# First loads on the software DMA queue, first FFN steps by token tile, and more transposes on TensorE in a linear-attention + SwiGLU kernel

## The chip, the cores and the metric

The kernel runs on one core of a Trainium2 chip. The metric is the device time of one execution in microseconds (us). The engines of the core are TensorE (PE), VectorE (DVE), ScalarE (ACT), GpSimd (POOL) and SyncE (SP). DMAs are issued by SP (hardware queue) or by POOL (software queue). PEld is PE's loading of weights.

## The reference

Cosine-weighted linear attention over 8 batches, 8 heads, 576 positions and 64 dimensions, then RMS normalization and a SwiGLU feed-forward network (FFN) with 512 model and 1536 inner dimensions on the 4608 tokens:

```python
q_p = phi(q, cos_w, sin_w)      # phi: concat(relu(x)*cos, relu(x)*sin): 128 features
k_p = phi(k, cos_w, sin_w)
kv  = einsum('bhsf,bhsd->bhfd', k_p, v);  z = sum(k_p, axis=2)
x   = einsum('bhsf,bhfd->bhsd', q_p, kv) / (einsum('bhsf,bhf->bhs', q_p, z) + 1e-06)
xn  = x / sqrt(mean(x * x) + 1e-06) * rms_g
out = (silu(xn @ w_gate) * (xn @ w_val)) @ w_out
```

All inputs and the output are float32; the kernel multiplies in bf16.

## The kernel before, in words

Each batch has 512 "main" tokens (four tiles `j` of 128) and 64 rest tokens; the rest tokens of all batches make a ninth FFN block, `xnT8`. The order of the work is written out by hand: every engine executes its instructions in the order of the program text.

**Attention of a batch.** `load_piece` brings `raw` (q, k or v; 1 MB) and the 64 rest rows (`remq`, `remk`, `remv`). `q_prep(b, j)` scales a tile by cos and sin into `qp` and transposes it into `qpT`, either with a DMA transpose on SP or, with `on_pe`, by eight PE transposes into a PSUM tile and a copy. `k_prep` and `v_prep` fill `kp` and `vv`. `kvz(b, half)` is 20 matmuls per half and a copy to `kvzs`. `nd(b, j)` makes numerator and denominator of tile `j` in PSUM (pool `att`). `x_of(b, j)` computes `den`, `rec` and `xt` on DVE, the sum of squares (`scr`, `ssq`) on ACT, and `ms` and `rs` on POOL. `xn` scales the tile on DVE and transposes it into `xnT`, by DMA or (`xn_pe`, and the head's `xn0`) by four PE transposes into `tpx` and a copy on ACT. `qr_prep` and `nd(b, NJ)` do the rest tokens of two batches at a time.

**FFN of a block.** `gval(blk, nn)`, twelve steps: four gate matmuls (`gps`) and four value matmuls (`vps`), 512 tokens wide, then `sil` on ACT and `hT` on DVE. `outp` (for block 0 the loop behind L474) accumulates over the twelve `hT` into `acc`; `store` copies it to `osb` (three buffers) on ACT and issues the output DMA on SP.

**Order.** The head loads batch 0 on SP, lets POOL wait for v (`gate`) before the weights, and does the attention of batch 0. Then come the twelve steps of block 0 with batch 1's scaling beside them, the output phase of block 0 with batch 1's attention, and blocks 1 to 8. In block `blk`, `attention_beside(blk + 1, nn)` and its two companions place the work of the next three batches beside step `nn`; block 1 has no `outp`.

Of the kernel before, what the change touches and what calls it, by code (L numbers as in the profile page):

```python
# [10 lines left out]
FP32 = mybir.dt.float32  # L11
# [6 lines left out]
def kernel(  # L18
# [28 lines left out]
    EPS = 1e-6  # L47

# [6 lines left out]
    xt_pool = ctx.enter_context(tc.tile_pool(name="xt", bufs=5))  # L55
# [13 lines left out]
    vv = consts.tile([P, NJ + 1, H, DE], BF16, name="vv")  # L69
    qpT = consts.tile([P, H, SM], BF16, name="qpT")  # L70
# [16 lines left out]
    def load_piece(what, src, b, h0, n, eng):  # L87
# [58 lines left out]
    def q_prep(b, j, e_cos=nc.vector, e_sin=nc.vector, on_pe=False):  # L146
# [3 lines left out]
        if on_pe:  # L150
            tps = pools["tps"].tile([P, H, P], BF16, name="tps", tag="tps")
            for h in range(H):
                nc.tensor.transpose(tps[:, h, :], qp[:, h, :], ident[:, :])
            return tps
# [37 lines left out]
    xts = {}  # L192
    xnTs = {}
# [20 lines left out]
    def x_of(b, j):  # L214
# [9 lines left out]
        xt = xt_pool.tile([P, DM], FP32, name="xt", tag="xt")  # L224
        nc.vector.tensor_tensor(  # L225
            out=xt[:, :].rearrange("p (g h d) -> p g h d", g=2, d=D),
# [4 lines left out]
        scr = ffn_pool.tile([P, DM], BF16, name="scr", tag="scr", bufs=1)  # L231
        ssq = small.tile([P, 1], FP32, name="ssq", tag="ssq")
        nc.scalar.activation(out=scr[:, :], in_=xt[:, :], func=AF.Square, accum_out=ssq[:, :])  # L233
        ms = small.tile([P, 1], FP32, name="ms", tag="ms")
        nc.gpsimd.tensor_scalar(  # L235
            out=ms[:, :], in0=ssq[:, :], scalar1=1.0 / DM, scalar2=EPS, op0=ALU.mult, op1=ALU.add
        )
        rs = small.tile([P, 1], FP32, name="rs", tag="rs")
        nc.gpsimd.tensor_tensor(out=rs[:, :], in0=ms[:, :], in1=mhalf[:, :], op=ALU.pow)  # L239
        xts[b, j] = (xt, rs)  # L240

    def xn(b, j, tps=None):
        xt, rs = xts.pop((b, j))
        if j < NJ:
            if b not in xnTs:
                xnTs[b] = xnt_pool.tile([P, NDT, SM], BF16, name="xnT", tag="xnT")
            dst, col = xnTs[b], j
        else:
            xnTs[B] = xnT8
            dst, col = xnT8, b // 2  # L250
        t = xn_pool.tile([P, DM], BF16, name="xn", tag="xn")
        nc.vector.scalar_tensor_tensor(  # L252
            out=t[:, :], in0=xt[:, :], scalar=rs[:, 0:1], in1=gb[:, :], op0=ALU.mult, op1=ALU.mult
        )
        if tps is not None:
            for dt in range(NDT):
                nc.tensor.transpose(tps[:, dt, :], t[:, dt * P : (dt + 1) * P], ident[:, :])  # L257
        else:
            nc.sync.dma_start_transpose(out=dst[:, :, col * P : (col + 1) * P], in_=t[:, :])
# [82 lines left out]
    for s in range(0, DFF, 512):  # L342
        load_wgv(s)
# [195 lines left out]
```

## Time and profile before

| | |
|---|---|
| median of 3 runs | 384.48 us (379.05 to 385.63) |
| profiled execution | 384.23 us, its span 382.5 us |
| PE busy | 325.6 us (85%) |
| DVE busy | 199.5 us (52%) |
| ACT busy | 147.9 us (39%) |
| POOL busy | 101.8 us (27%) |
| chain that ended last | PE 61%, DMA 12%, DVE 9%, issue 7%, POOL 5%, ACT 3% |
| granted PE clock, mean | 0.959 |
| moved by DMA | 54.65 MB, of them HBM read 38.01, written 9.44 |

Times in the rows are us from the span's start. A row of the timeline has start, duration, engine, source line, operation, output and input, count, and in brackets how long the engine stood idle before it and what released it. SPq and POOLq rows are the issuing of DMAs. The chain of work that ended last follows each instruction back to what released it; a DMA in it lasts from its issue to its landing.

### The profile page before, as it was taken

The page shows a single profiled execution, that of the slowest core. Times are in us where ns is not written, and L with a number is a line of the kernel's source. Part 1 is how long each engine was busy: PE and PEld are TensorE (multiplying, and loading weights), DVE is VectorE, ACT ScalarE, POOL GpSimd, SP SyncE. Part 2 cuts the span into 40 slices and gives each one's busy share as a digit, 9 for nine tenths or more (in the row PEclk, how much of TensorE's full clock was granted, in tenths as well). Part 3 has the DMA queues.
Part 4 walks back from the last instruction along what each step waited for, and adds up shares of the span by engine and source line. Part 5 has one row for each costly group of instructions (what it writes and reads, how often), then busy time and mean ns, then how long its engine had stood idle before and what let it go on. Part 6 is the DMA issues. An engine that isn't in the chain of part 4 may idle for free.

```text
span 382.5 us, 5536 instructions
## 1 busy us (share of the span) xinstructions
PE 325.6 (85%) x1979; PEld 158.2 (41%) x2016; DVE 199.5 (52%) x426; ACT 147.9 (39%) x295; POOL 101.8 (27%) x176
## 2 busy tenths in 40 slices
PE   0456996569855799989999997999999999999995
PEld 0342443233422254445445543444454444444442
DVE  2653592529467426963784684568737422222210
ACT  2724360435333434443445342534534433233221
POOL 0428410380046005731570375037002000000000
PEclk9999999996965799999999999899999999999999
DMA  7899999169055604896699289969902210000113
GB/s 224 211 204 235 291 322 251 38 203 277 1 137 147 130 29 110 166 225 161 164 235 247 74 172 174 164 157 208 240 27 70 55 55 28 27 29 38 45 48 92
DMA packets 69181, 54.65 MB, mean 143 GB/s; under 512 B 50688, under 2 KB 58368, under 8 KB 69152
## 3 DMA queue, kind: packets, MB, share of 16 engines
q0 software_dynamic: 12192, 29.50, 32.1%
q1 hardware_dynamic: 56816, 24.52, 29.1%
q8 instruction: 16, 0.26, 0.3%
q10 hardware_dynamic: 144, 0.26, 0.2%
q14 instruction: 13, 0.11, 0.1%
HBM read 38.01 MB, written 9.44 MB: 124 GB/s over the span
## 4 chain that ended last, share of the span: by engine, by line
PE 61%; DMA 12%; DVE 9%; issue 7%; POOL 5%; ACT 3%; SPq 2%; ACTq 0%; DVEq 0%; POOLq 0%
PE vps L273 19%; PE gps L273 19%; PE acc L303 17%; DMA raw<-in_v_dram 6%; DMA qpT<-qp 5%; DVE xt L225 2%; PE kvz L181 2%; PE nd L208 2%; DVE xn L252 2%; POOL raw L91 2%; POOL rs L239 2%; DMA out_dram<-osb 1%; DVE hT L279 1%; DVE kp L124 1%; SPq L98 1%
## 5 line engine op out<-in xcount | busy, mean ns | idle before, releaser
L279 DVE TENSOR_TENSOR hT<-vps,sil 128x512 bf16<-128x512 f32 x108 | 74.3, 688 | 137.2 <-PE vps L273 97.0
L273 PE MATMUL vps<-xnT,wv 128*128 128x512 bf16 x379 | 104.3, 399 | 3.6 <-ACT osb L285 3.2
L273 PE MATMUL gps<-xnT,wg 128*128 128x512 bf16 x366 | 101.3, 396 | 6.0 <-ACT sil L278 3.3
L303 PE MATMUL acc<-wo,hT 128*128 128x512 bf16 x374 | 96.2, 381 | 0.6
L278 ACT ACTIVATE sil<-gps 128x512 bf16<-128x512 f32 x108 | 63.9, 592 | 76.3 <-PE gps L273 73.1
L273 PEld LDWEIGHTS <-wv 128*128 128x128 bf16 x432 | 43.8, 101 | 59.2 <-issue 11.8
L273 PEld LDWEIGHTS <-wg 128*128 128x128 bf16 x432 | 40.8, 101 | 50.1 <-issue 11.5
L303 PEld LDWEIGHTS <-hT 128*128 128x128 bf16 x384 | 37.7, 98 | 46.2 <-issue 1.4
L235 POOL TENSOR_SCALAR ms<-ssq 128x1 f32<-128x1 f32 x36 | 7.3, 203 | 169.8 <-ACT scr L233 169.8
L233 ACT ACTIVATE scr<-xt 128x512 bf16<-128x512 f32 x36 | 22.7, 630 | 70.0 <-DVE xt L225 69.0
L285 ACT COPY osb<-acc 128x512 f32<-128x512 f32 x36 | 20.8, 585 | 30.6 <-PE acc L303 25.0
L252 DVE SCALAR_TENSOR_TENSOR xn<-xt,rs,gb 128x512 bf16<-128x512 f32 x36 | 26.6, 743 | 2.1 <-POOL rs L239 2.1
L225 DVE TENSOR_TENSOR xt<-nd,rec 128x512 f32<-128x512 f32 x36 | 24.9, 691 | 1.2
L131 ACT CAST vv<-raw 128x512 bf16<-128x512 f32 x28 | 16.0, 623 | 17.3 <-DMA raw<-in_v_dram 17.3
L239 POOL TENSOR_TENSOR rs<-ms,mhalf 128x1 f32<-128x1 f32 x36 | 21.0, 582 | 3.0
L257 PE MATMUL tpx<-ident,xn 128*128 128x128 bf16 x48 | 6.2, 272 | 17.0 <-DVE xn L252 17.0
L181 PE MATMUL kvz<-vv,kp 128*128 128x65 bf16 x320 | 14.1, 199 | 7.4 <-DVE vv L133 3.4
L208 PE MATMUL nd<-kvzs,qpT 128*128 128x65 bf16 x256 | 14.5, 202 | 5.7 <-DVE xt L225 3.0
L208 PEld LDWEIGHTS <-qpT 128*128 128x128 bf16 x256 | 12.8, 103 | 14.3 <-issue 5.6
L124 DVE TENSOR_SCALAR qp<-raw,cos_tab 128x512 bf16<-128x512 f32 x32 | 15.1, 477 | 5.7 <-DMA raw<-in_q_dram 5.7
L181 PEld LDWEIGHTS <-kp 128*128 128x128 bf16 x320 | 12.9, 101 | 11.5 <-issue 3.6
L91 POOL DMA_DIRECT2D raw<-in_k_dram x22 | 17.0, 772 | 2.3 <-DVE kp L124 2.3
(59 smaller groups left out, 225.6 us busy)
## 6 DMA issues: line engine op xcount, KB each, us to landing
out_dram<-osb SPq DMA_DIRECT2D x32, 256.0 KB, 3.6
raw<-in_q_dram POOLq DMA_DIRECT2D x20, 256.0 KB, 6.8
raw<-in_k_dram POOLq DMA_DIRECT2D x20, 256.0 KB, 3.8
raw<-in_v_dram POOLq DMA_DIRECT2D x20, 256.0 KB, 4.3
raw<-in_q_dram POOLq DMA_DIRECT2D x2, 1024.0 KB, 11.8
raw<-in_k_dram POOLq DMA_DIRECT2D x2, 1024.0 KB, 13.0
raw<-in_v_dram POOLq DMA_DIRECT2D x2, 1024.0 KB, 15.5
wg<-in_moe_w_gate_dram POOLq DMA_DIRECT2D x3, 512.0 KB, 9.0
```

The lines of the kernel that those rows point to most:

```text
L91: eng.dma_start(out=raws[what, b][:, h0 : h0 + n, :], in_=src[b, h0 : h0 + n, 0:SM, :].rearrange("h (p j) d -> p h (j d)", j=NJ),)
L181: nc.tensor.matmul(ps[:, half, hh * DE : (hh + 1) * DE], lhsT=kp[:, c, h, :], rhs=vv[:, c, h, :], start=(c == 0), stop=(c == NJ),)
L208: nc.tensor.matmul(ps[rows, h // HH, (h % HH) * DE : (h % HH + 1) * DE], lhsT=src[:, h, cols], rhs=kz[:, h, :], start=True, stop=True,)
L225: nc.vector.tensor_tensor(out=xt[:, :].rearrange("p (g h d) -> p g h d", g=2, d=D), in0=ndv[:, :, :, 0:D], in1=rec[:, :].rearrange("p (g h ...
L233: nc.scalar.activation(out=scr[:, :], in_=xt[:, :], func=AF.Square, accum_out=ssq[:, :])
L239: nc.gpsimd.tensor_tensor(out=rs[:, :], in0=ms[:, :], in1=mhalf[:, :], op=ALU.pow)
L252: nc.vector.scalar_tensor_tensor(out=t[:, :], in0=xt[:, :], scalar=rs[:, 0:1], in1=gb[:, :], op0=ALU.mult, op1=ALU.mult)
L273: nc.tensor.matmul(ps[:, :], lhsT=w[:, dt, nn * P : (nn + 1) * P], rhs=xnT[:, dt, :], start=(dt == 0), stop=(dt == NDT - 1),)
L278: nc.scalar.activation(out=sil[:, :], in_=gps[:, :], func=AF.Silu)
L279: nc.vector.tensor_tensor(out=hT[:, nn, :], in0=vps[:, :], in1=sil[:, :], op=ALU.mult)
L285: nc.scalar.copy(out=osb[:, :], in_=acc[:, :])
L303: nc.tensor.matmul(acc[:, :], lhsT=hTs[blk][:, nn, j * P : (j + 1) * P], rhs=wo[:, nn, :], start=(nn == 0), stop=(nn == NNT - 1),)
```

## The change

Five edits. (1) The first loads: half of batch 0's q stays on SP in two pieces, the other half, k, v and the weights go to POOL's queue, without the wait for v; the gain vector goes from ACT to SP; `load_rest` makes the rest rows a DMA of its own. (2) FFN steps 0 and 1 of block 0 are computed tile by tile: `first_steps(j)` does both steps for the 128 tokens of tile `j` right after that tile's transposes. (3) Batch 1's q tiles are transposed on PE, and its scaled `xn` tiles wait one step before PE transposes them; the same for batch 2's `xn` tiles, in a placement of its own (`batch2_beside`), with half of batch 2's q and k scaling on ACT. Batch 1's rest tokens move from the output phase to block 1. (4) `ms` goes: `xt` has a 513th column with the constant sqrt(EPS*512), the square is scaled by 512**-0.5, and `rs` is one power on POOL. `xt` is a ring of five fixed tiles. (5) The head's PSUM pools of its own go: `gv`, `acc` and `att` (one buffer) are used from the start.

The diff, cut:

```diff
-        if h0 + n == H:
...
+    def load_rest(what, src, b, eng):
+        lane = 64 * (b % 2) if what == "q" else 0
+        t = rem_pool.tile([P, H, D], FP32, name="rem" + what, tag="rem" + what)
+        eng.dma_start(
+            out=t[lane : lane + SR, :, :], in_=src[b, :, SM:S, :].rearrange("h s d -> s h d")
+        )
+        raws[what + "r", b] = t
...
+    def q_tr_pe(b, j, eng):
+        qp = qps.pop((b, j))
+        tps = pools["acc"].tile([P, H, P], BF16, name="tps", tag="acc")
+        for h in range(H):
+            nc.tensor.transpose(tps[:, h, :], qp[:, h, :], ident[:, :])
+        copy(eng, qpT[:, :, j * P : (j + 1) * P], tps[:, :, :])
...
-        nc.gpsimd.tensor_scalar(
-            out=ms[:, :], in0=ssq[:, :], scalar1=1.0 / DM, scalar2=EPS, op0=ALU.mult, op1=ALU.add
+        nc.scalar.activation(
+            out=scr[:, :], in_=xt[:, :], func=AF.Square, scale=DM**-0.5,
+            accum_out=ssq[:, :],
         )
-        nc.gpsimd.tensor_tensor(out=rs[:, :], in0=ms[:, :], in1=mhalf[:, :], op=ALU.pow)
+        nc.gpsimd.tensor_tensor(out=rs[:, :], in0=ssq[:, :], in1=mhalf[:, :], op=ALU.pow)
...
+    def gval_mm(blk, nn, c0, n):
...
+        for ps, w in zip(gv_ps[blk, nn], (wg, wv)):
             for dt in range(NDT):
                 nc.tensor.matmul(
-                    ps[:, :], lhsT=w[:, dt, nn * P : (nn + 1) * P], rhs=xnT[:, dt, :],
-                    start=(dt == 0), stop=(dt == NDT - 1),
+                    ps[:, c0 : c0 + n], lhsT=w[:, dt, nn * P : (nn + 1) * P],
+                    rhs=xnTs[blk][:, dt, c0 : c0 + n], start=(dt == 0), stop=(dt == NDT - 1),
                 )
...
+    load_piece("q", q, 0, 0, 2, nc.sync)
+    load_piece("q", q, 0, 2, 2, nc.sync)
+    load_piece("q", q, 0, HH, HH, nc.gpsimd)
...
+    load("k", k, 0)
+    load("v", v, 0)
...
+    xn_scale(0, 1)
+    xn_tr_pe(0, 1)
+    first_steps(0)
+    x_of(0, 3)
+    xn_scale(0, 2)
+    xn_tr_pe(0, 2)
+    first_steps(1)
+    xn_scale(0, 3)
+    xn_tr_pe(0, 3)
+    first_steps(2)
+    first_steps(3)
+    gval_end(0, 0)
+    gval_end(0, 1)
...
+        if 8 <= r <= 11:
+            xn_tr_pe(2, r - 8)
+        if 7 <= r <= 10:
+            xn_scale(2, r - 7)
+        if 6 <= r <= 9:
+            nd(2, r - 6)
+            x_of(2, r - 6)
...
-        if 5 <= nn <= 8:
-            q_prep(1, nn - 5)
+        if 6 <= nn <= 9:
+            q_scale(1, nn - 6, V, A)
+        if 8 <= nn <= 11:
+            q_tr_pe(1, nn - 8, V if nn % 2 else A)
```

**POOL at the start of the program**, before (`gate` reads v and so waits for it; `wg` and `wv` are the weights):

```order
L320 IOTA iota_i 128x1
masks.py:197 MEMSET ident 128x128
masks.py:199 AFFINE_SELECT ident<-ident 128x128
L341 COPY gate<-raw 128x1
L108 DMA wg<-in_moe_w_gate_dram 128x4x512
L108 DMA wv<-in_moe_w_val_dram 128x4x512
```

and POOL at the same place now:

```order
L91 DMA raw<-in_q_dram 128x4x256
L359 ISA
L359 IOTA iota_i 128x1
masks.py:197 MEMSET ident 128x128
masks.py:199 AFFINE_SELECT ident<-ident 128x128
L91 DMA raw<-in_k_dram 128x8x256
L100 DMA remk<-in_k_dram 64x8x64
L91 DMA raw<-in_v_dram 128x8x256
L100 DMA remv<-in_v_dram 64x8x64
L114 DMA wg<-in_moe_w_gate_dram 128x4x512
L114 DMA wv<-in_moe_w_val_dram 128x4x512
```

Half of q stands ahead of the iota and the identity, k and v behind them, and the weights follow at once.

**SP from its first load to batch 2's q**, before (`qpT` of four tiles is batch 1's, of eight batch 2's and batch 3's; `xnT_102` holds the rest tokens):

```order
L91 DMA raw<-in_q_dram 128x8x256
L98 DMA remq<-in_q_dram 64x8x64
L91 DMA raw<-in_k_dram 128x8x256
L98 DMA remk<-in_k_dram 64x8x64
L91 DMA raw<-in_v_dram 128x4x256 x2
L98 DMA remv<-in_v_dram 64x8x64
L155 DMA_TRANSPOSE qpT<-qp 128x8x128 x4
L166 DMA_TRANSPOSE qprT<-qpr 128x8x128
L288 DMA out_dram<-osb 128x512 x4
L259 DMA_TRANSPOSE xnT_102<-xn 128x4x128
L155 DMA_TRANSPOSE qpT<-qp 128x8x128 x8
```

and SP's rows now, to the same place:

```order
L91 DMA raw<-in_q_dram 128x2x256 x2
L363 DMA gb<-in_moe_rms_g_dram 128x512
L184 DMA_TRANSPOSE qprT<-qpr 128x8x128
L332 DMA out_dram<-osb 128x512 x4
L162 DMA_TRANSPOSE qpT<-qp 128x8x128 x4
L281 DMA_TRANSPOSE xnT_104<-xn 128x4x128
L162 DMA_TRANSPOSE qpT<-qp 128x8x128 x4
```

Batch 1's four q transposes are gone from SP; batch 2's still stand behind the four stores of block 0, and the rest tokens' transpose has moved behind them.

**DVE in the second half of block 1**, a step of the loop before (`hT` of the step, then tile 2 of batch 2, then batch 3's q and k):

```order
L279 TENSOR_TENSOR hT<-vps,sil 128x512
L218 TENSOR_SCALAR den<-nd 128x8
L223 RECIPROCAL rec<-den 128x8
L225 TENSOR_TENSOR xt<-nd,rec 128x512
L252 SCALAR_TENSOR_TENSOR xn<-xt,rs,gb 128x512
L124 TENSOR_SCALAR qp<-raw,cos_tab 128x8x64
L124 TENSOR_SCALAR qp<-raw,sin_tab 128x8x64
L124 TENSOR_SCALAR kp<-raw,cos_tab 128x8x64
L124 TENSOR_SCALAR kp<-raw,sin_tab 128x8x64
```

and a step at the same place now:

```order
L319 TENSOR_TENSOR hT<-vps,sil 128x512
L266 SCALAR_TENSOR_TENSOR xn<-xt_96,rs,gb 128x512
L237 TENSOR_SCALAR den<-nd 128x8
L242 RECIPROCAL rec<-den 128x8
L245 TENSOR_TENSOR xt_97<-nd,rec 128x512
L130 TENSOR_SCALAR qp<-raw,cos_tab 128x8x64
L130 TENSOR_SCALAR qp<-raw,sin_tab 128x8x64
L130 TENSOR_SCALAR kp<-raw,cos_tab 128x8x64
L130 TENSOR_SCALAR kp<-raw,sin_tab 128x8x64
```

`xn` stands ahead of `den` to `xt`. It scales the tile of the step before, and PE transposes it one step later still; before, PE's transposes in a step took the `xn` of that same step.

More of the change, by code (lines that the diff above doesn't have):

```diff
@@ L149, in q_prep, with q_tr @@
         relu_scaled(e_sin, qp[:, :, D:F], main("q", b, j), sin_tab, j, slice(0, P))
[L150 to L154, printed above, removed]
+        qps[b, j] = qp
+    def q_tr(b, j):
+        qp = qps.pop((b, j))
         nc.sync.dma_start_transpose(
@@ L449, in attention_beside @@
             x_of(b, NJ)
[L450 to L452 removed]
+        if 4 <= r <= 7:
             xn(b, r - 4)
```

262 lines of the change are left out of this document (138 added, 124 removed).

## The prediction

> **What bounds the kernel now.** I read the busy time by phases first, then the chain of work that ended last and the timeline in the phases where TensorE (PE) waits.
>
> ```profile
> 34.00:56.00 22.00, 21.73 (x93) 9.62 (x95) 13.47 (x27) 9.37 (x16) 9.79 (x13) 1.00 1.09 304
> 56.00:80.00 24.00, 15.66 (x152) 8.15 (x153) 11.66 (x28) 8.58 (x21) 6.24 (x13) 1.00 0.61 138
> 80.00:129.00 49.00, 33.66 (x181) 15.01 (x185) 29.10 (x65) 18.06 (x38) 16.45 (x27) 0.76 0.66 168
> 128.98:382.00 253.02, 243.36 (x1436) 116.24 (x1463) 128.50 (x260) 96.78 (x195) 57.60 (x100) 0.99 0.52 116
> ```
>
> The window rows give the busy time of PE, its weight loads, VectorE (DVE), ScalarE (ACT) and GpSimd (POOL), then granted clock, DMA share and GB/s. From 129 us on PE is busy 243.4 of 253.0 us: nothing there is to be had but its waits. What can move lies before: 34 us until the first gate matmul (33.95 below), 24 us for batch 0's output phase with PE busy 15.7, and 49 us for block 1 at a clock of 0.76. The change touches just these, so I sum them phase by phase.
>
> ```profile
> 9.08 1.33 ACT L122 ACTIVATE qp<-raw,sin_tab 128x512 bf16<-128x512 f32 x2 [6.21 <-DMA raw<-in_q_dram]
> 15.39 1.01 ACT L131 COPY qpT<-tps 128x1024 bf16<-128x1024 bf16 x1 [1.37 <-PE tps L153]
> 18.76 1.13 ACT L131 CAST vv<-raw 128x512 bf16<-128x512 f32 x2
> 22.86 0.43 DVE L133 CAST kvzs<-kvz 128x260 bf16<-128x260 f32 x1 [3.31 <-PE kvz L181]
> 33.95 0.58 PE L273 MATMUL gps<-xnT,wg 128*128 128x512 bf16 x1 [0.67 <-ACT xnT L131]
> 39.03 1.03 PE L273 MATMUL gps<-xnT,wg 128*128 128x512 bf16 x4
> 41.79 0.86 PE vps L273 x4
> 4.00:14.00 10.00, 2.42 (x22) 2.16 (x23) 2.36 (x5) 3.55 (x5) 0.00 (x0) 1.00 1.10 331
> 14.77 0.95 POOL L108 DMA_DIRECT2D wg<-in_moe_w_gate_dram  x1
> 16.00:18.00 2.00, 0.00 (x0) 0.10 (x1) 2.00 (x5) 2.00 (x4) 2.00 (x3) 1.00 0.57 61
> 35.00:37.00 2.00, 2.00 (x6) 0.72 (x5) 0.00 (x0) 0.60 (x1) 2.00 (x4) 1.00 1.02 399
> ```
>
> **Head, to FFN step 2 (39.03 us before).** ACT works without a long pause from q's landing (9.08) to the last vv cast (19.89): 10.8 us, of which q's part ends at 16.40, 7.3 us after q landed. v's landing does not set the end. Two things shorten it. First, q's 1 MB goes over two queues and only 512 KB of it shares SP's. The DMA engines are full from 4 to 14 us in both kernels (331 GB/s, share 1.10), so total bytes come hardly sooner, and 399 GB/s on POOL's queue at 35 us is the most it may gain. But q now stands ahead of everything: about 0.5 MB by 4 us, the whole by 5, and as before about 2 us from last bytes to the compute, so 7 instead of 9.08. Second, three scalings now precede the first transposes, and ACT's four (0.66 us each) no longer alternate with its copies: q's part takes about 5.9 us. So it ends at 12.9 (16.40 before). The k and v parts on ACT (3.5 us, 16.40 to 19.89) start at once if k has landed: q, gain vector and k are 2.3 MB, 9.3 us plus 2, so 11.3. They end at 16.5, **−3.3 us**. Bounds: 0 (the loads land as before and hide it) and −5 (k at 9.5).
>
> On POOL's queue the first half of q goes ahead of iota and identity (about 0.8 us later, idle until q lands), and k, v and the weights follow without the wait for v. The rest of q stands behind all weights and v's landing (about 14.5); the four rs behind it are wanted only past 22. The five one-column memsets lie in DVE's idle time before q. The gain vector moves to SP and is wanted past 22 too.
>
> From the last kvzs copy (23.29) to step 2 it took 15.74 us. Call this point T. By hand, with one `att` buffer instead of two: nd and the normalization chain of the four tiles end with xn of tile 3 at about T+9.3 as before (the missing ms saves 0.27 per tile, by 157.04 below; the single buffer gives it back). New is that steps 0 and 1 run under that wait: each tile brings 16 matmuls of 128 columns, 1.8 us cold (4 cold ones of that width take 0.61 at 110.48 below, with their tail) and 1.0 warm. Tiles 0 and 1 are hidden; behind the last transposes stand tiles 2 and 3. Step 2 starts at T+12.6, **−3.1 us**; if the narrow matmuls cost 1.6 each, −1.9.
>
> **FFN of batch 0, steps 2 to 11.** PE is the bound (21.73 of 22). Added are 4 times 8 transposes; 4 warm ones take 0.40 with their tail (72.75 below), so 8 take 0.5: **+2.0 us**, or 3.8 at half clock. The copies (0.69 on DVE, 1.01 on ACT) and the sines moved to ACT fit: ACT has 9.37 of 22 in use, and its fullest step holds 0.6 + 0.66 + 1.01 = 2.3 us against PE's 2.2.
>
> ```profile
> 56.30 0.81 PE L480 MATMUL acc<-wo,hT 128*128 128x512 bf16 x3
> 47.77 17.42 DMA qpT<-qp
> 60.12 0.77 PE L181 MATMUL kvz<-vv,kp 128*128 128x65 bf16 x20
> 62.22 0.43 DVE L133 CAST kvzs<-kvz 128x260 bf16<-128x260 f32 x1 [3.57 <-PE kvz L181]
> 65.24 0.43 PE L208 MATMUL nd<-kvzs,qpT 128*128 128x65 bf16 x8 [2.26 <-DMA qpT<-qp]
> 70.45 0.42 PE L208 MATMUL nd<-kvzs,qpT 128*128 128x65 bf16 x8 [0.45 <-DVE xt L225]
> 72.75 0.40 PE L257 MATMUL tpx<-ident,xn 128*128 128x128 bf16 x4 [1.88 <-DVE xn L252]
> 80.16 1.02 PE L273 MATMUL gps<-xnT,wg 128*128 128x512 bf16 x4 [0.30 <-ACT osb L285]
> 80.13 5.28 DMA out_dram<-osb
> 86.15 1.86 PE L273 MATMUL vps<-xnT,wv 128*128 128x512 bf16 x4 [3.24 <-ACT osb L285]
> ```
>
> **Output phase of batch 0 (56.30 to 80.16, 23.9 us).** Batch 1's first nd waited for a DMA transpose issued 17.42 us earlier. On PE that wait goes. What is late next is kvz: ACT's backlog of kp and vv (3.1 us) lets it start at +3.5, kvz and its copies take 2.5 (60.12 to 62.65 before), so nd of tile 0 is at +6.0 instead of +8.9. Three more tiles at the 1.74 us spacing of 65.24 to 70.45 put tile 3 at +11.2. Behind it are 0.43, five groups of four acc matmuls (0.86) and four transposes (0.39), 6.3 us together, then a copy and the first osb: +18.5. The batch's odd rows (`nd(1, NJ)`) go to block 1. **−5.4 us**; −3 if kvz and the x chain wait as long as before.
>
> ```profile
> 108.04 0.69 DVE L279 TENSOR_TENSOR hT<-vps,sil 128x512 bf16<-128x512 f32 x1 [0.56 <-ACT sil L278]
> 108.65 0.15 DVE L218 TENSOR_SCALAR den<-nd 128x8 f32<-128x8 f32 x1
> 109.07 0.69 DVE L225 TENSOR_TENSOR xt<-nd,rec 128x512 f32<-128x512 f32 x1
> 109.68 0.74 DVE L252 SCALAR_TENSOR_TENSOR xn<-xt,rs,gb 128x512 bf16<-128x512 f32 x1
> 110.34 0.48 DVE L124 TENSOR_SCALAR qp<-raw,cos_tab 128x512 bf16<-128x512 f32 x1
> 110.74 0.48 DVE L124 TENSOR_SCALAR qp<-raw,sin_tab 128x512 bf16<-128x512 f32 x1
> 110.48 0.61 PE L257 MATMUL tpx<-ident,xn 128*128 128x128 bf16 x4 [3.23 <-DVE xn L252]
> 117.05 0.61 PE L257 MATMUL tpx<-ident,xn 128*128 128x128 bf16 x4 [2.11 <-DVE xn L252]
> 107.00:129.00 22.00, 12.74 (x56) 5.46 (x54) 13.79 (x31) 7.70 (x17) 9.73 (x16) 0.61 0.69 167
> 128.98 1.43 PE L273 MATMUL gps<-xnT,wg 128*128 128x512 bf16 x4 [0.67 <-ACT xnT L131]
> 111.09 1.71 PE gps L273 x4
> 157.04 0.19 POOL L235 TENSOR_SCALAR ms<-ssq 128x1 f32<-128x1 f32 x1 [1.51 <-ACT scr L233]
> 157.31 0.68 POOL L239 TENSOR_TENSOR rs<-ms,mhalf 128x1 f32<-128x1 f32 x1
> 157.96 2.29 POOL L91 DMA_DIRECT2D raw<-in_v_dram  x3
> 166.25 1.14 ACT L131 CAST vv<-raw 128x512 bf16<-128x512 f32 x2 [5.09 <-DMA raw<-in_v_dram]
> ```
>
> **Block 1 (80.16 to 128.98, 48.8 us).** Its second half is a ring: PE's transposes wait for xn, xn stands on DVE behind hT of the same step, hT waits for that step's matmuls, and they stand behind the previous transposes. At half clock a turn took 6.57 us (110.48 to 117.05). Afterwards PE transposes what DVE scaled one step earlier, so the ring is cut and each step takes its fullest engine. By the starts above DVE takes 0.61 for hT, 1.03 for den to xt, 0.66 for xn, 0.40 for a qp or kp. Steps 0 to 11 are then 2.7, 2.1, 3.0, 3.0 (ACT: two kp of 0.67 and two vv of 0.57 as at 9.08 and 18.76, and sil like a vv), 2.5, 2.5, 2.2, 3.1, 3.9, 3.9, 2.9, 2.4: 34.2, and 1 more where xn waits for rs. Two waits remain. The fourth osb still needs the first store: three buffers, landing 5.28 us before amid 2 MB of loads; now `rs` of the odd rows holds most of those loads back behind ACT, so I take 3 us (0 to 5.3). And v of batch 3: its last piece now follows the last rs of batch 2 by one step, 5 us before the cast that wants it; the like in block 2 landed 8.3 us after issue (157.96 to 166.25). I take 3 us (1.5 to 5.2). Together 41, **−7.8 us**. The four DMA transposes of batch 2's q stand on SP behind the fourth store, about +5, and are wanted at step 6, about +17; in the trace such four took 7 us with loads beside them, so they cost nothing; with the 17.42 of batch 1 they would cost 5.
>
> **From block 2 on.** Only ms goes (0.27 us, 157.04 to 157.31): it counts where POOL's next v piece is late, in blocks 2 and 4: **−0.5**.
>
> **Sum.** −3.3 −3.1 +2.0 −5.4 −7.8 −0.5 = −18.1. The profiled execution took 384.23 us (span 382.5), the median of the runs 384.48: 366.
>
> **A rule against it.** The engines' share of 1.10 above says that they were full when SP issued. The Trainium skill (DMA: Bandwidth & Descriptors, Issuing engines are not separate DMA queues) says that transfers of all issuing engines run on the same 16 engines, and only issue time is saved; the trace agrees for the bytes. The same page (SWDGE vs HWDGE vs iDMA, and the table of latencies) gives a first byte after about 1 us on this queue against 0.6 on SP's; by it the sum would be 0.4 us higher, as an estimate.
>
> **Rivals.**
> *The loads land no sooner.* The engines are full, and POOL's first weights of 14.77 us moved only 61 GB/s from 16 to 18 us, a slow start that q's second half and k would share. Then the −3.3 falls away: 369.4. This is also what the skill's rule on issuing engines would give.
> *The waits are hidden.* If neither store nor v stops block 1, 6 us more go: 360.
> *Late q transposes in block 1*, as at 47.77: +5, 371.
> *Half clock in block 1.* The clock fell after 3.2 us without matmuls (before 110.48) and after 3.6 (before 86.15), not after the 2.3 before 65.24. The v wait may be long enough, and steps at 55% PE work may not bring it back. Twelve steps of 3.45 (two groups of 1.71 as at 111.09) and 7 us of attention matmuls are 48.4 instead of 35, partly over the two waits: +10, 376.
> *Slower: half clock already from step 2 of batch 0.* If the 128-column steps and their gaps do not count as work, ten steps at 3.45 instead of 1.73 (two groups of 0.86 as at 41.79) add 17.3, and block 1 its 10: 393. It decides if PE's gaps reach some 3 us in each stretch after T. Against it: after the first matmuls at 33.95 the clock was up by 39.03.
>
> **Numbers.** Chances: the forecast 0.40, no sooner loads 0.18, hidden waits 0.14, late transposes 0.08, half clock in block 1 0.14 (half of it past the bound), half clock throughout 0.06. Two per cent, about what a measurement of this kernel can tell from no change, is 376.8 to 392.2. Faster: 0.40 + 0.18 + 0.14 + 0.08 + 0.07 = 0.87; within 0.07; slower 0.06. The range is from 357 (hidden waits, k early and less in the output phase) to 377 (half clock in block 1).
>
> **What would show it.** First q scaling at about 7, last vv cast near 16.5, step 2 at 32 to 33; first acc matmul near 52, first gate matmul of block 1 near 70, of block 2 near 111; no turn of 6.57 us; waits of ACT for a store and for v inside block 1. Wrong would be: q after 9, a clock near 0.6 in block 1, or block 2 starting past 120.

## The result and the profile after

The changed kernel took 369.8 us in the median (369.28 to 372.0, four runs) where the kernel before took 383.16 (379.05 to 385.63, four runs): a ratio of 0.9697 with a 95% interval of 0.9598 to 0.9796. The ratio compares fast runs alone, so it leaves out the slow 385.63, while the medians take in every run. The prediction was 366.0 with a range of 357 to 377. The profiled execution took 370.0 us, its span 368.2; that of before 384.23 and 382.5. So 14.3 us went in the profiled pair where 18.1 were forecast.

The window rows of the changed kernel, cut at its own first matmuls (columns as in the prediction: PE, its weight loads, DVE, ACT, POOL, then clock, DMA share, GB/s):

```profile
4.00:14.00 10.00, 3.71 (x32) 3.29 (x32) 5.30 (x16) 4.40 (x7) 5.64 (x8) 1.00 0.94 277
35.22:54.27 19.05, 19.05 (x112) 9.60 (x112) 12.30 (x22) 11.74 (x19) 7.36 (x10) 1.00 1.14 285
54.27:71.49 17.22, 14.98 (x139) 7.76 (x137) 10.70 (x25) 8.94 (x21) 3.63 (x6) 1.00 0.81 185
71.49:115.27 43.78, 28.48 (x201) 13.24 (x201) 26.23 (x57) 23.11 (x48) 16.72 (x24) 0.92 0.73 154
115.27:368.20 252.93, 243.67 (x1464) 116.02 (x1463) 130.62 (x263) 96.50 (x195) 53.22 (x77) 0.99 0.57 121
```

The ten steps of block 0 are filled by PE, the output phase nearly so (15.0 of 17.2). Block 1 is still the place with PE idle: 28.5 of 43.8 us. The timeline of ACT and DVE in the head and of PE and ACT in block 1 shows the starts that the prediction had named:

```profile
8.54 2.56 ACT L128 ACTIVATE qp<-raw,sin_tab 128x512 bf16<-128x512 f32 x4 [4.49 <-DMA raw<-in_q_dram]
13.18 1.80 DVE L130 TENSOR_SCALAR kp<-raw,cos_tab 128x512 bf16<-128x512 f32 x4 [0.31 <-DMA raw<-in_k_dram]
17.43 1.14 ACT L137 CAST vv<-raw 128x512 bf16<-128x512 f32 x2 [0.73 <-DMA raw<-in_v_dram]
21.61 0.43 DVE L139 CAST kvzs<-kvz 128x260 bf16<-128x260 f32 x1 [2.92 <-PE kvz L199]
...
74.06 0.58 ACT L329 COPY osb<-acc 128x512 f32<-128x512 f32 x1 [1.64 <-DMA out_dram<-osb]
84.71 0.19 PE L199 MATMUL kvz<-vv,kp 128*128 128x65 bf16 x1 [1.51 <-ACT vv L137]
85.75 0.19 PE L199 MATMUL kvz<-vv,kp 128*128 128x65 bf16 x1 [0.85 <-ACT vv L137]
87.44 0.64 PE L199 MATMUL kvz<-vv,kp 128*128 128x65 bf16 x16 [1.50 <-ACT vv L137]
87.92 1.82 PE L310 MATMUL gps<-xnT,wg 128*128 128x512 bf16 x4
113.11 1.14 ACT L137 CAST vv<-raw 128x512 bf16<-128x512 f32 x2 [4.30 <-DMA raw<-in_v_dram]
```

q's first scaling starts at 8.54 and v's cast waits for v until 17.43. In block 1 ACT waits 1.64 us for the store, PE waits three times for ACT's vv before kvz, a group of four gate matmuls then takes 1.82 us instead of 1.03, and ACT waits 4.30 us for v of batch 3. Before, the wait for the store was longer:

```profile
85.52 0.58 ACT L285 COPY osb<-acc 128x512 f32<-128x512 f32 x1 [4.43 <-DMA out_dram<-osb]
```

The chain of work that ended last names the transfers that still count:

```profile
4.51 12.89 DMA raw<-in_v_dram
71.47 2.49 DMA out_dram<-osb
108.58 4.51 DMA raw<-in_v_dram
145.34 6.49 DMA raw<-in_v_dram
206.83 3.51 DMA remk<-in_k_dram
216.16 20.17 DMA qpT<-qp
248.51 8.10 DMA raw<-in_v_dram
```

In the head it is v of batch 0 that counts: it lands at 17.40, and from there the chain goes through ACT's vv casts and kvz to the last kvzs copy. The store takes 2.49 us instead of 5.28. The q transposes of batch 1, 17.42 us before, are gone; such a transpose of a later batch now appears.

### The profile page after: what moved, and what is told of

It reads as the page before. It is cut to its first block, busy times and chain, and to the rows that moved or that the text cites. A ratio compares the mean times of both kernels' runs of the same rounds, so it can differ in the third digit from the quotient of the medians.

```text
span 368.2 us, 5681 instructions
## 1 busy us (share of the span) xinstructions
PE 322.9 (88%) x2096; PEld 161.3 (44%) x2096; DVE 197.2 (54%) x420; ACT 156.5 (43%) x310; POOL 98.0 (27%) x145
## 4 chain that ended last, share of the span: by engine, by line
PE 56%; DMA 16%; DVE 12%; ACT 8%; issue 4%; POOL 2%; ACTq 0%; SPq 0%; DVEq 0%; POOLq 0%
PE gps L310 17%; PE vps L310 17%; PE acc L347 15%; DMA raw<-in_v_dram 9%; DMA qpT<-qp 5%; PE kvz L199 3%; DVE hT L319 3%; ACT sil L318 2%; PE nd L227 2%; ACT scr L253 2%; ACT vv L137 2%; DVE kp L130 2%; POOL raw L91 1%; PE acc L546 1%; DVE rec L242 1%
## 5 line engine op out<-in xcount | busy, mean ns | idle before, releaser
L310 PE MATMUL gps<-xnT,wg 128*128 128x512 bf16 (+1 forms) x408 | 102.3, 376 | 7.2 <-ACT xnT L137 5.0
L310 PE MATMUL vps<-xnT,wv 128*128 128x512 bf16 (+1 forms) x408 | 102.4, 376 | 0.0
L258 POOL TENSOR_TENSOR rs<-ssq,mhalf 128x1 f32<-128x1 f32 x36 | 20.4, 566 | 167.3 <-ACT scr L253 167.3
L310 PEld LDWEIGHTS <-wg 128*128 128x128 bf16 x456 | 41.9, 100 | 48.2 <-issue 9.6
L137 ACT CAST vv<-raw 128x512 bf16<-128x512 f32 x28 | 16.2, 623 | 20.3 <-DMA raw<-in_v_dram 20.3
L227 PE MATMUL nd<-kvzs,qpT 128*128 128x65 bf16 x256 | 14.3, 200 | 8.7 <-DMA qpT<-qp 2.5
L227 PEld LDWEIGHTS <-qpT 128*128 128x128 bf16 x256 | 12.3, 102 | 17.1 <-DMA qpT<-qp 3.0
L130 DVE TENSOR_SCALAR qp<-raw,cos_tab 128x512 bf16<-128x512 f32 x32 | 16.6, 528 | 3.2 <-issue 3.2
L91 POOL DMA_DIRECT2D raw<-in_q_dram x23 | 17.7, 775 | 1.1 <-POOLq L589 0.8
L91 POOL DMA_DIRECT2D raw<-in_v_dram x23 | 17.5, 761 | 1.9 <-DMA wo<-in_moe_w_out_dram 1.4
L130 DVE TENSOR_SCALAR kp<-raw,cos_tab 128x512 bf16<-128x512 f32 x32 | 15.6, 502 | 0.4 <-DMA raw<-in_k_dram 0.3
L170 PE MATMUL tps<-ident,qp 128*128 128x128 bf16 x64 | 6.2, 262 | 9.5 <-ACT qp L128 9.3
L310 PE MATMUL vps<-xnT_104,wv 128*128 128x512 bf16 x48 | 12.3, 379 | 0.0
## 6 DMA issues: line engine op xcount, KB each, us to landing
raw<-in_v_dram POOLq DMA_DIRECT2D x3, 1024.0 KB, 16.2
```

Of the source, the lines that this page charges most:

```text
L91: eng.dma_start(out=raws[what, b][:, h0 : h0 + n, :], in_=src[b, h0 : h0 + n, 0:SM, :].rearrange("h (p j) d -> p h (j d)", j=NJ),)
L130: nc.vector.tensor_scalar(out=dst, in0=src, scalar1=tab[lanes, col : col + 1], scalar2=0.0, op0=ALU.mult, op1=ALU.max,)
L137: nc.scalar.copy(out=dst, in_=src)
L227: nc.tensor.matmul(ps[rows, h // HH, (h % HH) * DE : (h % HH + 1) * DE], lhsT=src[:, h, cols], rhs=kz[:, h, :], start=True, stop=True,)
L258: nc.gpsimd.tensor_tensor(out=rs[:, :], in0=ssq[:, :], in1=mhalf[:, :], op=ALU.pow)
L310: nc.tensor.matmul(ps[:, c0 : c0 + n], lhsT=w[:, dt, nn * P : (nn + 1) * P], rhs=xnTs[blk][:, dt, c0 : c0 + n], start=(dt == 0), stop=(dt ...
```

## The experiments

Times are medians. One table gives the phases of all profiled executions, each a difference of two starts in its trace: "first q" is ACT's first scaling, T the end of the last kvzs copy, then T to step 2, steps 2 to 11 of block 0, its output phase, block 1, and the rest of the span.

| kernel | median us | first q | T | T to step 2 | steps | output phase | block 1 | rest |
|---|---|---|---|---|---|---|---|---|
| before | 383.16 | 9.08 | 23.29 | 15.74 | 17.27 | 23.86 | 48.82 | 253.52 |
| changed | 369.80 | 8.54 | 22.04 | 13.18 | 19.05 | 17.22 | 43.78 | 252.93 |
| a0_again | 369.16 | 9.08 | 22.37 | 11.99 | 19.05 | 17.22 | 43.04 | 252.93 |
| e1_sp_loads | 368.51 | 9.85 | 22.83 | 13.01 | 19.06 | 17.21 | 43.95 | 249.94 |
| e2_wide_steps | 372.67 | 8.89 | 22.52 | 16.89 | 19.05 | 17.21 | 44.26 | 252.87 |
| e3_q1_dma | 381.31 | 10.27 | 22.96 | 12.05 | 17.26 | 29.53 | 44.45 | 254.65 |
| e4_batch2_old | 370.03 | 8.52 | 22.01 | 12.35 | 19.05 | 17.21 | 46.13 | 251.55 |
| e5_q_sp_gate | 372.82 | 12.75 | 25.57 | 12.65 | 19.05 | 17.22 | 43.64 | 249.97 |
| e6_vv_dve | 369.05 | 9.51 | 22.31 | 12.97 | 19.05 | 17.22 | 42.76 | 255.09 |
| e7_pieces_early | 366.14 | 8.27 | 21.45 | 12.26 | 19.05 | 17.21 | 42.02 | 248.21 |
| e9_early_osb4 | 358.37 | 8.33 | 21.20 | 11.95 | 19.05 | 17.22 | 38.21 | 248.77 |
| e10_osb4 | 367.50 | 8.80 | 21.99 | 12.56 | 19.05 | 17.22 | 42.56 | 253.62 |
| e11_best | 359.74 | 9.41 | 22.50 | 12.35 | 19.05 | 17.21 | 38.41 | 248.48 |
| e12_q_alone | 371.78 | 7.60 | 22.77 | 12.56 | 19.05 | 17.22 | 43.65 | 253.85 |

The steps and the output phase do not move unless they are edited. T moves with the landing of the loads, and the rest by some us from execution to execution: 249.9 to 255.1 in kernels that leave it alone. T to step 2 takes 11.95 to 13.18 in the twelve profiles with narrow steps 0 and 1. In all of them the first narrow gate matmul starts at T+6.85; what differs is when PE goes from half to full clock. Window rows show the granted clock (third column from the right) on both sides of that moment, first in the changed kernel's first profile, then in `a0_again`, the same program:

```profile
28.89:33.11 4.22, 4.22 (x41) 4.22 (x41) 1.92 (x3) 1.89 (x4) 2.92 (x5) 0.50 0.72 128
33.48:35.20 1.72, 1.72 (x31) 1.60 (x29) 0.00 (x0) 1.09 (x3) 1.72 (x3) 1.00 0.97 357
```

```profile
29.22:31.28 2.06, 2.06 (x21) 2.06 (x20) 1.24 (x3) 1.30 (x3) 0.77 (x3) 0.51 0.73 146
31.28:34.30 3.02, 3.02 (x55) 2.95 (x53) 0.67 (x1) 1.76 (x4) 3.02 (x5) 1.00 0.56 115
```

A group of four narrow matmuls takes 0.43 us from start to start at half clock and 0.22 at full, in these profiles and in the others. Full clock comes at T+11.4 in the first profile and at T+8.9 in the second. So 1.2 us of this phase depend on the execution and not on the program.

### The changed kernel once more

> The changed kernel as it is, beside the other three, to have their differences on one chip. Expected: 369.3 to 370.3 as before, block 1 43.5 to 44.5 us long. If the runs of one kernel differ by some 2 us from chip to chip, then the 1.3 us by which the version with SP's loads came out ahead cannot be told from no difference.

369.16 us (368.39 to 371.34), ratio to before 0.9642 (0.9573 to 0.971). A kernel's median comes back within 0.7 us; differences below that are not read.

### First loads back on SP

```diff
-    load_piece("q", q, 0, 0, 2, nc.sync)
-    load_piece("q", q, 0, 2, 2, nc.sync)
-    load_piece("q", q, 0, HH, HH, nc.gpsimd)
...
-    load("k", k, 0)
-    load("v", v, 0)
+    load_piece("q", q, 0, 0, H, nc.sync)
+    load_rest("q", q, 0, nc.sync)
+    load_piece("k", k, 0, 0, H, nc.sync)
...
+    nc.gpsimd.tensor_copy(out=gate[:, :], in_=raws["v", 0][:, 0, 0:1])
```

> The changed kernel (369.8 us), with its first loads put back: q, k and v of batch 0 on SP in the old order, the weights on POOL behind the wait for v, the gain vector from ACT. Theory: moving the loads brought almost nothing, because the software queue moved 277 GB/s from 4 to 14 us where SP's moved 331, and the 1.25 us that the stretch to the last kvzs copy became shorter came from putting three scalings ahead of the first transposes. Then q's first scaling is at about 9.1 again, the last kvzs copy at 22 to 22.6, and the time 369.5 to 370.5. Rival A: the whole 1.25 us is the loads', so 371.1. Rival B: the software queue costs more than it brings (v's cast waited until 17.43 although v had landed by 14.6 before), so the last kvzs copy comes before 21.5 and the time is 368 to 369.

368.51 us (367.76 to 368.68), ratio 0.9624 (0.9564 to 0.9685). No theory got all of it. The head's window row:

```profile
4.00:14.00 10.00, 3.21 (x31) 2.96 (x32) 2.87 (x6) 3.57 (x5) 0.00 (x0) 1.00 1.11 283
```

SP's queue alone moved 283 GB/s here, not the 331 of before, so the 277 of the changed kernel (271 to 286 in the nine profiles with its head) is no slower. q lands 1.3 us later than in the changed kernel's first profile, T comes at 22.83, 0.8 later, and the time is none the worse, since the rest of the span is 3 us shorter. What shortened the rest is open; its waits for v and for DMA transposes differ from profile to profile. T itself can be read in two parts. From ACT's first scaling to T it took 14.21 us before, 12.98 here, 13.09 in `e11_best` below, which has these loads too, and 12.69 to 13.63 in nine profiles with the changed head. So the new order of scalings and transposes alone brings about 1.2 us, as far as one profile of before can tell, and that is the size of the head's 1.25. The first scaling itself starts at 9.08 before, at 9.85 and 9.41 with the loads on SP, and at 8.27 to 10.27, in the median at 8.80, with the changed head. A gain from the new place of the loads is within that scatter and is not shown.

### Steps 0 and 1 in full width

```diff
-        for nn in range(2):
-            gval_mm(0, nn, j * P, P)
...
-    gval_end(0, 0)
-    gval_end(0, 1)
+    gval(0, 0)
+    gval(0, 1)
```

> The changed kernel with FFN steps 0 and 1 of block 0 in full width behind the last transposes, as before the change. Theory: the 2.56 us by which the way from the last kvzs copy to step 2 became shorter are the tiles 0 and 1 of these steps, run under the wait for xn. So that way takes 15.2 to 16.2 us again instead of 13.2, and the time is 372 to 373. Rival: PE's narrow matmuls at the cold clock (0.43 per four) are as dear as what they hide, and the gain is that of the missing ms: the way stays at 13 to 13.7 us, the time 369.5 to 370.3.

372.67 us (371.89 to 374.59), 3 us slower, as the theory said; the way from T to step 2 is 16.89, longer than the 15.2 to 16.2 expected. PE's timeline of this kernel shows why:

```profile
35.10 1.91 PE L310 MATMUL vps<-xnT,wv 128*128 128x512 bf16 x4
36.80 1.90 PE L310 MATMUL gps<-xnT,wg 128*128 128x512 bf16 x4
38.51 1.06 PE L310 MATMUL vps<-xnT,wv 128*128 128x512 bf16 x4
39.41 1.03 PE L310 MATMUL gps<-xnT,wg 128*128 128x512 bf16 x4
```

Here steps 0 and 1 start behind the last transposes, at T+10.9, and three of their four groups, the two of 1.9 us among them, run at half clock by these times (the profile's clock column does not show it here). Tile by tile the first gate matmul comes at T+6.85, under the wait for xn, and much of the half-clock stretch falls into time in which PE would wait anyway.

### Batch 1's q by DMA transposes

```diff
-        if 8 <= nn <= 11:
-            q_tr_pe(1, nn - 8, V if nn % 2 else A)
+            q_tr(1, nn - 6)
```

> The changed kernel with batch 1's four q tiles transposed by DMA on SP again, each right behind its scaling (steps 6 to 9), and not on PE. Theory: the ten steps of block 0 lose the 1.8 us that the PE transposes cost, and the output phase waits for the DMA transposes again, which took 17.42 us before: issued at about 45 to 52 and landing near 65, against first nd at 60.55 now. The output phase becomes 5 to 7 us longer, in all +3 to +5: 373 to 375. Rival: with the load in flight shorter they land by 60; then only the 1.8 us go, and the time is 367.5 to 368.5.

381.31 us (377.92 to 383.04), ratio to before 0.9973 (0.9929 to 1.0017): with this one edit undone nearly nothing of the gain is left. The steps of block 0 give back exactly the 1.8 us of the theory (17.26), but the output phase takes 29.5 us, 12.3 more and not 5 to 7. PE's timeline of this kernel, a row of its chain, and its window row for the phase:

```profile
62.82 0.62 PE L227 MATMUL nd<-kvzs,qpT 128*128 128x65 bf16 x8 [4.32 <-DMA qpT<-qp]
71.22 0.62 PE L227 MATMUL nd<-kvzs,qpT 128*128 128x65 bf16 x8 [6.07 <-DMA qpT<-qp]
```

```profile
46.80 24.38 DMA qpT<-qp
```

```profile
58.00:70.00 12.00, 2.83 (x15) 0.88 (x13) 1.23 (x4) 0.72 (x2) 0.56 (x1) 0.69 1.12 233
```

The transpose that the chain names took 24.38 us from issue to landing, 17.42 before, with the engines' share at 1.12 beside it. PE is busy 2.8 of 12 us at a mean clock of 0.69. So the DMA path costs more here than it did before; the DMA issues from 40 to 75 us show the four of each kernel (count, median us from issue to landing), before and then here:

```profile
qpT<-qp SPq DMA_TRANSPOSE x4, 11.0
```

```profile
qpT<-qp SPq DMA_TRANSPOSE x4, 16.4
```

In both the loads of one batch's q, k and v are issued in this window, and they too were slower, 21.0 to 21.7 us to their landing against 17.0 to 17.7 before, while the engines moved as much (230 and 227 GB/s). What made the transfers take longer is not settled.

### Batch 2 as before in block 1

```diff
     def batch2_beside(r):
-        if r in (0, 1):
-            for j in (2 * r, 2 * r + 1):
-                q_scale(2, j, V, A)
-                q_tr(2, j)
...
-        if 8 <= r <= 11:
-            xn_tr_pe(2, r - 8)
...
+        if 5 <= r <= 8:
+            xn_scale(2, r - 5)
+            xn_tr_pe(2, r - 5)
```

> The changed kernel with batch 2's work in block 1 placed as before the change (scaling on DVE, xn transposed on PE in the step that scales it); batch 1's rest tokens stay in block 1. Theory: the 5.04 us that block 1 became shorter come from this placement alone, since in its second half PE's transposes no longer wait for the xn of their own step. So the turns of 6.6 us at half clock come back, block 1 takes 47.5 to 50 us, the time is 373.5 to 376. Rival: what made block 1 shorter is the wait for the store (4.43 before, 1.64 now) and the earlier loads; block 1 stays at 44 to 45.5 and the time at 370 to 371.5.

370.03 us (367.3 to 371.93). The time is the rival's; block 1 at 46.13 lies between the two. PE's waits from 60 to 320 us explain both, first those of the changed kernel, then those of this one (total, times, longest):

```profile
PE gps L310 <- ACT xnT L137: 5.0, 1, 5.0
PE tpx L287 <- DVE xn L266: 3.3, 4, 1.8
```

```profile
PE tpx L287 <- DVE xn L266: 8.9, 4, 3.2
PE gps L310 <- ACT xnT L137: 0.7, 1, 0.7
```

The new placement does cut the ring: the waits of PE's transposes for xn fall from 8.9 to 3.3 us. But the block then arrives early at the wait for v of batch 3, and PE's wait for the copy that stands behind it on ACT grows from 0.7 to 5.0. Of 5.6 us won 4.3 are given back at the end of the block. The other 2.7 us by which block 1 is shorter than before (48.82 to 46.13) are in this kernel too, and the store has their size: ACT's wait for it is 1.69 us instead of 4.43, and a row of the chain shows it taking 2.54 us instead of 5.28:

```profile
70.60 2.54 DMA out_dram<-osb
```

### The head: where q lands

```diff
-    load_piece("q", q, 0, 0, 2, nc.sync)
-    load_piece("q", q, 0, 2, 2, nc.sync)
-    load_piece("q", q, 0, HH, HH, nc.gpsimd)
+    for h0 in range(0, H, 2):
+        load_piece("q", q, 0, h0, 2, nc.sync)
...
+    nc.gpsimd.tensor_copy(out=gate[:, :], in_=raws["v", 0][:, 0, 0:1])
```

> The changed kernel with all of q on SP in four pieces of two heads, k and v on POOL's queue and the weights behind a wait for v. Theory: q's first scaling waits for the 512 KB piece on POOL's queue (8.54; it took 7.2 us from issue where SP's 256 KB pieces took 2.8), so with all of q on SP it starts at 6 to 7.5, and v, with no weights behind it in the queue, lets its casts start by 16.4. The last kvzs copy then ends at 20 to 21 instead of 22.04, and the time is 367.8 to 369. Rival: the 16 engines set the landing, whichever queue issues, and k and v come as late as now: the last kvzs copy stays at 21.7 to 22.5, and the later weights (FFN step 0 needs them at 28.9) may cost 0.5: 369.8 to 370.5.

372.82 us (370.13 to 373.94): both theories fell, as ACT's first row shows.

```profile
12.75 2.56 ACT L129 ACTIVATE qp<-raw,sin_tab 128x512 bf16<-128x512 f32 x4 [10.32 <-DMA raw<-in_q_dram]
```

The next kernel makes POOL wait for its half of q before it issues k:

```diff
+    nc.gpsimd.tensor_copy(out=gate[:, :], in_=raws["q", 0][:, HH, 0:1])
     load("k", k, 0)
```

> The changed kernel with POOL waiting for its half of q before it issues k, v and the weights, so that q has the DMA engines to itself. Theory: what held q's landing at 8.54 (7 predicted), and at 12.75 where all of q was on SP beside k on POOL, is the sharing of the engines with k; alone, q's 1 MB goes at some 300 GB/s and the first scaling starts at 6.3 to 7.3; k, issued at about 6.5 instead of 4, lands 1 to 2 us later than now, so that the last kvzs copy still ends at 22 to 23.5: 369.5 to 371. Rival: the software queue itself is slow to begin and to report, and q still starts ACT at 8 to 9; then everything behind it is later by the whole wait, the last kvzs copy ends at 24 to 26 and the time is 371.5 to 374.

ACT's first rows of it:

```profile
7.60 2.56 ACT L129 ACTIVATE qp<-raw,sin_tab 128x512 bf16<-128x512 f32 x4 [3.95 <-DMA raw<-in_q_dram]
14.38 2.56 ACT L129 ACTIVATE kp<-raw,sin_tab 128x512 bf16<-128x512 f32 x4 [0.95 <-DMA raw<-in_k_dram]
```

It took 371.78 us (370.47 to 372.9). With all of q on SP and k at once on POOL, q is ready at 12.75; on SP with k behind it in the same queue at 9.85 and 9.41; split over both queues with k behind POOL's half at 8.27 to 10.27 (nine profiles); with nothing beside it but the gain vector at 7.60. The first and the last stand outside the scatter, with one profile each; the two in the middle cannot be told apart. So what lands first depends on how the bytes are dealt to the two queues: the engines serve both, and k beside q takes part of the rate. The Trainium skill (DMA: Bandwidth & Descriptors, SWDGE vs HWDGE vs iDMA) says that an engine goes round-robin between its internal queues and that the two kinds of issue feed different ones; the 12.75 with k on the other queue and the 7.60 without k agree. But the sum is kept: with q alone, k comes at 14.38 and T at 22.77, as late as ever. The theory nearly held for q and held for T, but the time is 0.8 us above it, inside the rival's range; where that went is open.

### Block 1: the casts, the loads, the store

```diff
-                v_prep(2, c)
+                v_prep(2, c, V)
```

> The changed kernel with four of batch 2's vv casts (steps 2 and 3 of block 1) on DVE instead of ACT. Theory: block 1 gained 5 us and not 7.8 because ACT's backlog of kp and vv holds up kvz of batch 2 (PE waits 1.51, 0.85 and 1.50 us at 84.7 to 87.4) and brings half clock for one step (gps 1.82 at 87.92, sum of the loss some 5 us). On DVE, which has slack there, the casts come in time, both go, and block 1 takes 39 to 41.5 us instead of 43.8: 365.5 to 367.5. Rival: kvz then waits for DVE's kp instead, or the gained time is given back at the wait for v (108.58, 4.51 us): block 1 43 to 44 and 369 to 370.

369.05 us (365.9 to 371.18), the same as the 369.16 of the changed kernel on that chip. The theory fell to its rival: kvz waits for DVE now. PE's timeline of this kernel:

```profile
84.94 0.19 PE L199 MATMUL kvz<-vv,kp 128*128 128x65 bf16 x1 [1.24 <-DVE vv L139]
85.77 0.19 PE L199 MATMUL kvz<-vv,kp 128*128 128x65 bf16 x1 [0.64 <-DVE vv L139]
86.84 0.64 PE L199 MATMUL kvz<-vv,kp 128*128 128x65 bf16 x16 [0.89 <-DVE kp L130]
```

The last group starts at 86.84 instead of 87.44. In steps 2 to 4 ACT and DVE both have a backlog, and a cast moved from one to the other moves the wait.

```diff
-                    pieces[-14 + 4 * i + e] = (what, src, 2 * e, 2)
+                    pieces[-18 + 4 * i + e] = (what, src, 2 * e, 2)
```

> The changed kernel with the load pieces of batches 3 to 7 issued four steps earlier, so that v's pieces stand on POOL ahead of the four rs of the batch before and not between them. Theory: the waits for v (4.51 us at 108.58 with the half clock behind it, 6.49 at 145.34, 8.10 at 248.51 on the chain) come from issues that stand behind rs; with them gone block 1 takes 39 to 40.5 us, blocks 2 to 8 3 to 5 us less than 252.9, and the time is 360 to 364. Rival: the DMA engines, at shares of 0.9 to 1 in most of the middle, are the cause; then the waits only move (to the DMA transposes of q or to the output stores), and the time is 368 to 371.

366.14 us (361.97 to 368.98), between the two theories: 3 us faster by the medians, of runs that spread over 7, and nearer 5 by the ratios to before, 0.9517 (0.9423 to 0.9612) against 0.9642. Its profiled execution was the fastest, 361.97. In it, from block 1 on ACT waits for v no more, and the rest of the span is 4.7 us shorter (248.21) than in the changed kernel's profiles. Block 1 gains only 1 to 2 us (42.02), because the store comes back, as a row of ACT and one of the chain show:

```profile
75.07 0.58 ACT L329 COPY osb<-acc 128x512 f32<-128x512 f32 x1 [4.17 <-DMA out_dram<-osb]
```

```profile
69.95 5.02 DMA out_dram<-osb
```

With the loads issued ahead of the rs again the first store takes 5.02 us, as it took 5.28 before the change; held back behind the rs, it took 2.49. So the change, by holding the loads back, had bought a quick store with a late v. Two more kernels take ACT's wait for the store away, the first with this edit alone, the second with the earlier pieces as well:

```diff
-    osb_pool = ctx.enter_context(tc.tile_pool(name="osb", bufs=3))
+    osb_pool = ctx.enter_context(tc.tile_pool(name="osb", bufs=4))
```

> The changed kernel with four osb buffers and nothing else. Theory: the store wait (1.64 us on ACT at 74.06) goes, but block 1 ends when v of batch 3 lands, whose pieces follow rs and move up with the work; so about 1 to 2 us: block 1 41.5 to 43 us, 367.5 to 368.8. Rival: it is taken back whole by the wait for v, then 369 to 370; or the fourth buffer frees the loads to collide with other transfers, then 370 to 371.

> The version with the earlier load pieces (366.1 us), with four osb buffers instead of three, so that the fourth copy of batch 0's output waits for no store. Theory: in that version the wait for the first store grew from 1.64 to 4.17 us, because the loads that no longer stand behind rs now run beside the store; it sets ACT back, and ACT works without a pause from there to the kvzs copy. With the fourth buffer block 1 takes 38 to 39.5 us instead of 42.0, and the time is 361.5 to 364. Rival: kvz of batch 2 waits for DVE or for the loads themselves, then block 1 stays at 41 to 42.5 and the time at 365 to 367.

The fourth buffer alone: 367.5 us (366.46 to 368.77), ratio 0.9574 (0.9538 to 0.9611), about 2 us faster than the changed kernel, as expected, and block 1 at 42.56, with a wait of 4.07 us for v left on ACT. Both edits together: 358.37 us (357.28 to 359.51), ratio 0.9334 (0.9297 to 0.937), better than expected. Apart they are worth about 3 to 5 and 2 us, together 11. Block 1 and the rest of this kernel in window rows, and a stretch of PE's timeline:

```profile
69.42:107.63 38.21, 28.79 (x200) 13.58 (x200) 25.28 (x55) 23.02 (x48) 15.51 (x24) 0.91 0.94 185
107.63:356.40 248.77, 243.05 (x1464) 115.97 (x1463) 131.70 (x265) 97.41 (x195) 52.83 (x77) 0.99 0.59 121
```

```profile
80.97 0.19 PE L199 MATMUL kvz<-vv,kp 128*128 128x65 bf16 x1 [1.51 <-ACT vv L137]
82.01 0.21 PE L199 MATMUL kvz<-vv,kp 128*128 128x65 bf16 x1 [0.85 <-ACT vv L137]
83.70 1.04 PE L199 MATMUL kvz<-vv,kp 128*128 128x65 bf16 x16 [1.48 <-ACT vv L137]
84.55 1.90 PE L310 MATMUL gps<-xnT,wg 128*128 128x512 bf16 x4
```

Block 1 takes 38.2 us, and PE is busy 243.1 of the 248.8 that follow. The backlog before kvz, with its 3.8 us of waits and the step at half clock, is untouched: of the waits named so far, it is what is left in this block. Last, the same with the first loads on SP:

> The earlier load pieces, four osb buffers, and the first loads on SP in their old order. Theory: the first loads on SP are worth -0.6 to -1.3 us against the changed kernel (368.5 against 369.2 and 369.8), the other two edits -6 to -8, so 360.5 to 363.5. Rival: the place of the first loads is worth nothing, and this version is within 0.5 us of the one without it.

359.74 us (358.92 to 364.01), ratio 0.9388 (0.9336 to 0.9441): 1.4 us slower than without it, where a gain was expected. The intervals overlap. T (22.50 against 21.20) points the same way, but 21.20 is the earliest of the nine, so it is likely, not shown, that the changed head is the better one once the waits for v are gone. The fastest kernel measured is the changed one with the earlier pieces and the fourth buffer.

## Why the prediction was right, and where it was off

**The direction and the place.** Each phase moved to the side that the sum said, and the gain comes from the phases it named. The miss is 3.8 us: two terms gave 4.8 us less than forecast, T to step 2 0.5 less, and the output phase and the steps 1.5 more. The median of 369.8 lies nearest to 369.4, the rival of loads that land no sooner; only the phases tell the two apart.

**Head: −3.3 forecast, −1.25 measured, mis-sized.** The step on ACT held: from first scaling to the end of q's part it took 5.7 us (5.9 forecast). The landings failed: q at 8.54 instead of 7, k at 13.18 instead of 11.3, and v, which was said not to set the end, landed at 17.40 and did. The engines moved 277 GB/s from 4 to 14 us where the estimate took the 331 of before, and q, "ahead of everything", shared them with k; alone it was ready at 7.60. In nine profiles q came at 8.27 to 10.27, in three of them after 9, which the prediction itself had named as a sign of being wrong. On the loads the rival of no sooner landing was right in the main: no gain from them is shown, and the new order of the work is worth about 1.2 us by itself.

**T to step 2: −3.1 forecast, −2.56 in this profile.** The forecast way of 12.6 us lies amid the 11.95 to 13.18 of the profiles that have it, and the edit undone costs 3 us. Which of these a profile shows depends on when PE reached full clock, which the sum could not know.

**Steps 2 to 11: +2.0 forecast, +1.78 measured,** and back to 17.26 without the PE transposes.

**Output phase: −5.4 forecast, −6.64 measured.** nd of the four tiles was forecast at +6.0 to +11.2 us into the phase and ran as these rows of PE show, 6.3 to 11.3 after 54.27:

```profile
60.55 0.42 PE L227 MATMUL nd<-kvzs,qpT 128*128 128x65 bf16 x8
65.55 0.43 PE L227 MATMUL nd<-kvzs,qpT 128*128 128x65 bf16 x8 [0.41 <-DVE xt_97 L245]
```

What follows took 1.4 us less than forecast, in part because the sum laid the busy times of the rows end to end, 0.39 for four transposes: their tails overlap, and the next row on PE starts 0.23 us after they start. What the sum did not say is how much hung on this edit: against the same kernel without it, it is worth 11 to 12 us, most of the whole change.

**Block 1: −7.8 forecast, −5.04 measured, mis-sized.** By the starts of the gate matmuls, steps 0 to 3 took 9.3 us (13.8 forecast with 3 for the store, which cost 1.64), steps 4 and 5 took 11.2 (5.0), steps 6 to 10 took 14.3 (16.0), and step 11 took 9.0 (5.4 with 3 for v); the forecast had 1 us more for rs. Errors of 4 to 6 us stand against each other here, so that the sum of the block came out within 2.8 us is in part luck. Two steps of the argument failed. The list of "each step takes its fullest engine" let no backlog pass from step to step, but ACT carried its kp and vv from steps 2 and 3 to the kvz of step 4, where PE met it; moving casts to DVE showed that neither engine had the room. And step 11 had a wait of 4.30 us for v on ACT, not 3, and on PE 1.75 us more for xn before it; the half clock at the start of the next block came on top. The ring was cut as forecast (3.3 us of waits instead of 8.9, the slowest turn 3.9 us), yet the kernel with the old placement was as fast (370.03), since most of what the cut won went into the wait for v.

**The rest: −0.5 forecast, −0.59 in the profiles.** This is within the scatter of that phase (249.9 to 255.1 in kernels that leave it alone) and was not tried by itself.

Of the rivals, late q transposes of batch 2 and half clock through all of block 1 did not come; its clock was 0.92. The prediction's figure of 3.6 us for the pause before 86.15 is 3.24 by the row itself, and the changed kernel fell to half clock after shorter pauses than any that it lists. The rival of hidden waits, 360, is what came when both waits were taken away by `e9_early_osb4` (358.37). The slower case did not come near: the steps of block 0 ran at 1.00.

## What to carry to other kernels

An edit that cuts a ring of waits only pays up to the next transfer that is issued behind that work: look on each queue for what stands behind the instructions that you speed up, and move those issues with it. Two waits that hide each other, here a store and a load, are worth little one at a time and much together (3 to 5 and 2 us alone, 11 as a pair). When summing step by step the fullest engine, carry each engine's backlog into the next step.

## What the runs showed of the hardware

- DMA transposes beside loads have no stable time: the one on the chain took 17.42 us before, 24.38 when issued 1 us earlier in the program of the changed kernel, 20.17 in a later batch.
- A 256 KB store, the first of block 0, took 2.5 us on the chain with the loads held back, 5.28 with them beside it before, and 5.02 when only the loads were moved ahead again.
- A second queue did not add rate: from 4 to 14 us the engines moved 271 to 286 GB/s with the changed head (nine profiles), 331, 283 and 282 with SP's queue alone. What stands beside a load counts for its landing: q was ready at 12.75 on SP with k on POOL, at 7.60 with k held back, and at 8.27 to 10.27 split over both queues.
- PE dropped to half clock after three waits of 1.51, 0.85 and 1.50 us with single matmuls between them (82.7 to 87.9), not only after one long wait; with waits of 0.45, 1.24, 0.64 and 0.89 in `e6_vv_dve` it dropped too.
- The same tile-by-tile steps reached full clock at different times: 2.0 to 4.6 us after the first narrow gate matmul in twelve profiles, and step 2 started 11.95 to 13.18 us after T accordingly.
